# Leading pieces of the second unit's maxima: made ahead of the attention loop, or caught up inside its first twelve steps

## The chip, the cores and the metric

The kernel runs on one core of a Trainium2 chip. Five engines work beside each other and meet only at semaphores: PE (TensorE, matmuls, with PEld for the loading of the stationary operand), DVE (VectorE), ACT (ScalarE), POOL (GpSimd) and SP (SyncE, which here only issues DMAs). Each engine takes its instructions in order. The metric is the device time of one execution in microseconds. One execution was also recorded by the hardware profiler, and all times of single instructions come from that one.

## What is computed

Two independent heads, put side by side in the output. Head A is a long convolution (its kernel K is made from complex exponentials, the convolution is done by transforms). Head B is softmax attention without a mask, and it is in B that the change lies:

```python
def _B_ref(x, wqkv, wo):          # x [1, 2048, 448]
    H = 16; Dh = D // H           # 16 heads of 28
    qkv = (x @ wqkv).reshape(B, S, 3, H, Dh).transpose(2, 0, 3, 1, 4)
    q, k, v = qkv[0], qkv[1], qkv[2]
    scores = jnp.einsum("bhqd,bhkd->bhqk", q, k) * Dh ** -0.5
    p = _softmax(scores, axis=-1)
    o = jnp.einsum("bhqk,bhkd->bhqd", p, v)
    return o.transpose(0, 2, 1, 3).reshape(B, S, D) @ wo
```

All inputs and outputs are float32.

## The kernel before, in words

**Stages.** A first stage (lines 226 to 590) makes q, k and v and the seeds of head A's kernel, and ends with the row maxima of the first attention unit. Then one loop of NS = 256 steps (line 1045) does all of the attention, with the rest of head A spread over it as side jobs, and a tail finishes head A.

**Units and steps.** The 16 heads are four groups of four (G, HG). The 2048 query rows are four chunks of 512 (NQ). A unit u is one group and one chunk, 16 in all (NU); each has 16 steps (NK), one for every 128 keys. In a step, `s_mm` (line 753) makes the scores of 128 keys against 512 queries for each of the four heads (tile pss, a ring of three PSUM banks) and ACT turns each into p by an exponential; `pv_step` (line 760) multiplies the p of the step before with v into po.

**Maxima.** The exponential needs each row's maximum. It isn't subtracted afterwards: it is put as two extra rows into the query operand qhat, by `max_end` and `max_put` (lines 212 and 220: a PE transpose, two DVE operations that write mh, and two DMAs qhat<-mh), and the scores then come out with it taken off. So a unit's maxima must be finished before its first score. For that, `max_mm` (line 187) computes the scores of 128 query rows of one head against all 2048 keys once more, in four pieces kc = 0 to 3, each a matmul of 128x512 into one bank pm:

- kc 0: matmul with kdif (the difference of two halves of the keys), then ACT writes its relu into rl;
- kc 1: matmul with one of these halves, then DVE adds rl and takes the row maximum in one operation;
- kc 2 and 3: matmul with a quarter of the keys, then a DVE maximum (TENSOR_REDUCE).

The relu with the sum gives the elementwise maximum of both halves, so that three DVE passes do for four quarters. A unit needs 16 row blocks (i) of four pieces, 64 pieces. Step s of the loop makes the four pieces of block `sm = s + NK + LEAD` (blocks counted through all units), which is a unit and LEAD = 3 blocks ahead of the step itself. The first unit's maxima are made before the loop, and so are the three blocks of the second unit by which the loop is ahead (lines 906 to 908): 12 pieces. When a unit's last block is done, `max_join` and `max_end` follow.

**The order in a step** is written out by hand (line 34):

```python
ORDER = ('m0', 's0', 'm1', 's1', 'v', 'f', 'pv', 'f', 'v', 'k', 'm2', 's2', 'm3', 's3', 'v')
```

m is a piece of the maxima, s the scores of one head, pv the product with v. v is one DVE operation of head A (`vec`, from `g_powers`, tiles g and zg: nine per block, the first of them three short instructions). f is a side job of PE (`slot`, line 996): parts of head A's transforms (`u_part`, tiles ua, w to ub), the kernel's blocks (`k_mm`, tiles e, g to ko, and w, ko to yk), or what a finished unit still wants. k starts a block of head A's kernel (`k_begin`, `k_seed`) and hands POOL its next e operations. Within the loop all five engines keep exactly this program order (line 903).

**Banks.** PSUM's eight banks are ps_s with three for pss, ps_o with one for po, ps_g with one for zg, and three for pm. `w_tile` (line 125) hands the three out in turn, pm0, pm1, pm2, to the pieces of the maxima and to all side jobs alike. A matmul into a bank waits until what was there three takings before has been read out.

**Just before the loop** the order is: the first unit's maxima and their `max_end`, with the two puts on ACT's DMA queue; `load_sd(0)`, also on ACT's queue (sdb), and `load_sd(1)` and (2) on SP's; the twelve pieces; `k_seeds(0)` twice, which copies sdb on ACT into e and g for POOL and DVE; then step 0.

Of the kernel before, what the change touches and what calls it, by code (L numbers as in the profile page):

```python
# [26 lines left out]
NK = L // 128  # L27
# [4 lines left out]
NS = NU * NK  # L32
LEAD = 3
# [57 lines left out]
def body(ctx, tc, a, out):  # L91
# [5 lines left out]
    def pool(stack, name, bufs=1, space=None, side=None):  # L97
        kw = {} if space is None else {"space": space}
        if side:
            kw["side"] = side  # L100
        return stack.enter_context(tc.tile_pool(name=name, bufs=bufs, reuse_waits="tile", **kw))
# [23 lines left out]
    def w_tile():  # L125

        n_ring[0] += 1
        return ps_w[0].tile([128, CQ], F32, name=f"pm{n_ring[0] % ps_w[1]}")
# [16 lines left out]
    def load_k(g, j, p):  # L145
        if j == 0:
            t = k0_t if g == 0 else p.tile([128, HG, L], F32R, name="khat")
            kt_g[g] = [t[:, i] for i in range(HG)]
        for r in range(4):
            nc.sync.dma_start(kt_g[g][j][r::4, :].bitcast(F32), k_d[g][r % 2, 32 * j:32 * j + 32, :])  # L150
# [3 lines left out]
    def load_v(g, c):  # L154
        v_g[g, c] = t = v_p.tile([128, NK // NQ, HG, 32], F32, name="v", bufs=5)
        nc.sync.dma_start(t.rearrange("p t h e -> p t (h e)"), v_d[c][:, g])

    def load_kd(g, j, rows=range(4)):
        if 0 in rows:
            kd_g[g, j] = kd_p.tile([128, CQ], F32R, name=f"kdif{j}")  # L160
        t = kd_g[g, j]
        for r in rows:
            nc.sync.dma_start(t[r::4].bitcast(F32), kd_d[g][r % 2, 32 * j:32 * j + 32, :])

    def load_q(u, rows=range(4)):
        g, c = divmod(u, NQ)
        if 0 in rows:
            q_u[u] = q_p.tile([128, HG, CQ], F32R, name="qhat", bufs=3)
        t = q_u[u]
        for r in rows:  # L170
            nc.sync.dma_start(t[r::4].bitcast(F32), q_d[g][c][r // 2].rearrange("(j p) q -> p j q", j=HG))
# [15 lines left out]
    def max_mm(u, i, kc, ps=w_tile):  # L187

        if i == 0 and kc == 0:
            m_u[u] = q_p.tile([128, HG, 4, 3], F32, name="mx", bufs=2)  # L190
        j, t = divmod(i, 4)
        pm = ps()
        q, kt = q_u[u][:, j, t * 128:(t + 1) * 128], kt_g[u // NQ][j]
        mx = m_u[u][:, j, t, max(kc - 1, 0):max(kc - 1, 0) + 1]
        if kc == 0:
            nc.tensor.matmul(pm, q, kd_g[u // NQ, j], start=True, stop=True)
            rl_u[u, i] = kd_p.tile([128, CQ], F32, name="rl", bufs=2)
            nc.scalar.activation(rl_u[u, i], pm, AF.Relu)
        elif kc == 1:
            kb = kt.rearrange("p (c s n) -> p c s n", c=NQ, s=2)[:, :2, 1, :]  # L200
            nc.tensor.matmul(pm.rearrange("p (c n) -> p c n", c=2), q, kb, start=True, stop=True)
            rl = rl_u.pop((u, i))
            nc.vector.tensor_tensor_reduce(rl, pm, rl, 1.0, -3.0e38, ALU.add, ALU.max, mx)
        else:
            nc.tensor.matmul(pm, q, kt[:, kc * CQ:(kc + 1) * CQ], start=True, stop=True)
            nc.vector.tensor_reduce(mx, pm, axis=AX.X, op=ALU.max)
# [448 lines left out]
    def load_sd(b, queue=nc.sync):  # L655
        sds[b] = g_p.tile([128, SDF], F32, name="sdb", bufs=4)
        queue.dma_start(sds[b], sd_d[b // BO][b % BO])

    def k_seeds(b):

        if b not in es:
            es[b] = e = g_p.tile([128, 2, 16, N2], F32, name="e", bufs=2)
            nc.scalar.activation(e[:, :, :, :8], sds[b][:, :F_G].rearrange("p (c h e) -> p c h e", c=2, e=8), AF.Copy)
        else:
            g = g_p.tile([128, 2, 16, N1], F32, name="g", bufs=2)
            nc.scalar.activation(g[:, :, :, :4], sds[b][:, F_G:F_Z].rearrange("p (c h e) -> p c h e", c=2, e=4), AF.Copy)
            egs[b] = es.pop(b), g
# [85 lines left out]
    def s_mm(u, kt, j):  # L753
        pss = ps_s.tile([128, CQ], F32, name="pss")
        nc.tensor.matmul(pss, kt_g[u // NQ][j][:, kt * 128:(kt + 1) * 128], q_u[u][:, j, :], start=True, stop=True)
        p = kq_p.tile([128, CQ], F32, name="p", bufs=PB)
        nc.scalar.activation(p, pss, AF.Exp, scale=SCALE)
        return p
# [10 lines left out]
    def load_og(u):  # L769
        og_u[u] = og = kq_p.tile([128, G - 1, CQ], F32, name="og")  # L770
        nc.sync.dma_start(og, on_d[u % NQ][:G - 1].rearrange("g p q -> p g q"))
# [131 lines left out]
    nc.kept = KEPT["a"]  # L903
    for b in range(3):
        load_sd(b, nc.sync if b else nc.scalar)
    for i in range(LEAD):
        for kc in range(4):
            max_mm(1, i, kc)
    k_seeds(0)
    k_seeds(0)  # L910

# [84 lines left out]
    def slot(s_):  # L996
        n_slot[0] += 1
        if urgent and urgent[0][0] <= n_slot[0]:
            urgent.popleft()[2]()
        elif s_ >= NS and f_slot(s_, "s"):  # L1000
            pass
        elif p_due and p_due[0][0] <= s_:
            p_due.popleft()[1]()
        elif m_due and m_due[0][0] <= s_:
            m_due.popleft()[1]()
        elif u_due and u_due[0][0] <= s_:
            u_part(*u_due.popleft()[1:])
        else:
            f_slot(s_, "s") or f_slot(s_, "f")

    def k_seed(s_):
        b = k_due[0] if k_due else NB
        if b < NB and b not in egs and done["mm"] >= b - 2 and K0 + b * KP <= s_ + (1 if b in es else 2):
            k_seeds(b)
# [18 lines left out]
    def k_next():  # L1033

        if last[0] is not None and not powers["e"] and not powers["g"]:
            if last[0] + 3 < NB:
                load_sd(last[0] + 3)
            last[0] = None

    def vec():  # L1040
        if powers["g"]:
            powers["g"].popleft()()

    prev = None
    for s in range(NS):
        u, kt = divmod(s, NK)
        sm = s + NK + LEAD
        if s == 12 * NK:
            k0_st.close()
            f_p["s", 0] = f_p["s", 1] = pool(f0_st, "f0_p", side="right")  # L1050
            f_ready["s", 0], f_ready["s", 1] = s, NS
        if s >= 12 * NK and f_ready["s", 1] == NS and not (k_due or m_due or powers["g"] or powers["e"]):
            g_st.close()
            ps_st.close()
            ps_w[:] = pool(ps_st, "ps_f", 4, PSUM), 1
            f_ready["s", 1] = s + F1
        if kt == 12 and u // NQ == G - 1:
            load_og(u)
        late[0] = s + NK + LEAD > NS
        if u % NQ == NQ - 1 and u < NU - 1 and kt % 4 == 2:  # L1060
            load_v(u // NQ + 1, kt // 4)
        if sm < NS and sm // NK % NQ == NQ - 1 and sm % NK % 4 == 0 and sm % NK and sm // (NQ * NK) + 1 < G:
            load_kd(sm // (NQ * NK) + 1, sm % NK // 4 - 1)
        if sm < NS and sm % (NQ * NK) == 0 and sm:
            load_kd(sm // (NQ * NK), HG - 1)
        if kt % 4 == 1 and u % NQ == 1 and u // NQ + 1 < G:
            load_k(u // NQ + 1, kt // 4, k_pools[(u // NQ + 1) % 2])
        if kt == 2:
            if u + 2 < NU:
                load_q(u + 2)  # L1070
        ps = []
        for op in ORDER:
            if op[0] == "s":
                ps.append(s_mm(u, kt, int(op[1])))
            elif op[0] == "f":
                slot(s)
            elif op[0] == "v":
                vec()
            elif op == "k":
                k_next()  # L1080
                k_begin(s)
                k_seed(s)
                for _ in range(3):
                    if powers["e"]:
                        powers["e"].popleft()()
            elif op == "pv":
                if prev:
                    pv_step(*prev)
                    if prev[1] == NK - 1:
                        fin(prev[0], s)  # L1090
            elif sm < NS:
                max_mm(sm // NK, sm % NK, int(op[1]))
        for _ in range(FX if late[0] else 0):
            slot(s)
        if sm < NS and sm % NK == NK - 1:
            def end(un=sm // NK):
                max_end(un, w_tile())
                max_put(un)
            max_join(sm // NK)
            soon_slot(UG[0], end)  # L1100
        k_next()
        prev = (u, kt, ps)
    pv_step(*prev)
    fin(prev[0], NS)
    s = NS
# [63 lines left out]
```

## Time and profile before

| | us |
|---|---|
| median of three runs | 1278.88 |
| lowest and highest of them | 1276.07 and 1279.31 |
| the profiled execution | 1278.37 |
| its span, first to last instruction | 1276.6 |
| first score matmul of step 0 (from the span's start) | 228.65 |
| first score matmul of step 12 | 273.00 |

How to read the lines: times count from the span's start. PE, DVE, ACT, POOL and SP are the engines, a q behind a name is its instruction queue (waits, DMA issues). Almost all instructions carry L75, the line of a helper through which they are issued, so groups are told apart by their tiles: out<-in. In a row of the timeline stand start, duration, engine, operation, tiles, shape, how many, and in brackets the idle time before and what ended it. In a row of the windows stand the stretch, its length, then busy time and count of PE, PEld, DVE, ACT and POOL, the granted clock of TensorE, the share of the DMA engines and GB/s. In a row of the chain stand start, length and what held it.

### The profile page before, as it was taken

How to read it: one execution, taken by the hardware profiler on the slowest of the kernel's cores; microseconds unless marked ns; L12 is line 12 of the kernel's file. 1: busy time of each engine (PE TensorE's matmuls, PEld its weight loads, DVE VectorE, ACT ScalarE, POOL GpSimd, SP SyncE). 2: the span in 40 equal slices, each digit the busy share in tenths (PEclk: the TensorE clock that was granted, in tenths of full speed). 3: DMA queues.
4: the chain of work that ended last, by engine and by line, in shares of the span. 5: the costliest groups of instructions: out<-in, count | busy, mean ns of one | idle time of the engine just before them, and what ended most of it. 6: DMA issues, size and time to landing. Idle time of an engine off the chain costs nothing.

```text
span 1276.6 us, 33328 instructions
## 1 busy us (share of the span) xinstructions
PE 1223.9 (96%) x12641; PEld 699.3 (55%) x12641; DVE 923.0 (72%) x2106; ACT 967.5 (76%) x2162; POOL 846.2 (66%) x728
## 2 busy tenths in 40 slices
PE   7789887999999999999999999999999999999997
PEld 5667664555555555555555555555555545544433
DVE  6788866877777877877788888888897645645111
ACT  6878765788888888888878888888887666656452
POOL 2666750897788888878599999989995222324321
PEclk9889999899999999999999999999999999999999
DMA  7768699446564645375633133422324533657666
GB/s 216 244 223 288 233 304 346 113 93 186 160 149 113 168 119 168 113 235 167 176 94 104 49 88 97 154 81 71 88 54 156 179 131 135 204 170 228 198 170 167
DMA packets 200089, 205.36 MB, mean 161 GB/s; under 512 B 95992, under 2 KB 158520, under 8 KB 197880
## 3 DMA queue, kind: packets, MB, share of 16 engines
q1 hardware_dynamic: 199400, 202.63, 52.6%
q8 instruction: 100, 1.64, 0.5%
q10 hardware_dynamic: 528, 0.59, 0.2%
q14 instruction: 61, 0.50, 0.1%
HBM read 120.73 MB, written 82.18 MB: 159 GB/s over the span
## 4 chain that ended last, share of the span: by engine, by line
PE 75%; DVE 8%; POOL 6%; ACT 4%; issue 3%; DMA 3%; SPq 0%; ACTq 0%; POOLq 0%; DVEq 0%
PE pm L75 43%; PE pss L75 16%; PE po L75 16%; POOL e L75 2%; DVE tri L75 1%; ACT rl L75 1%; POOL qhat L75 1%; DVE mx L75 1%; DVE sg L75 1%; POOL eu L75 1%; ACT tri L75 1%; DVE px L75 1%; DVE qhat L75 1%; DVE hl L75 1%; DMA sd<-qhat 1%
## 5 line engine op out<-in xcount | busy, mean ns | idle before, releaser
L75 ACT ACTIVATE p<-pss 128x512 f32<-128x512 f32 x1024 | 561.0, 610 | 112.5 <-PE pss L75 107.2
L75 PE MATMUL pss<-qhat,khat 128*128 128x512 f32 x1024 | 403.2, 400 | 1.5 <-ACT p L75 1.4
L75 DVE TENSOR_REDUCE mx<-pm 128x1 f32<-128x512 f32 x480 | 308.6, 684 | 109.1 <-PE pm L75 107.2
L75 PE MATMUL pm<-khat,qhat 128*128 128x512 f32 x749 | 325.9, 438 | 6.4 <-ACT rl L75 4.2
L75 POOL TENSOR_TENSOR e<-e,sdb 128x256 f32<-128x256 f32 x168 | 201.8, 1201 | 110.6 <-ACT e L75 101.2
L75 PE MATMUL po<-p,v 128*32 128x512 f32 x2048 | 269.1, 594 | 0.0
L75 POOL TENSOR_TENSOR e<-e,eu 128x256 f32<-128x256 f32 x168 | 248.2, 1477 | 13.2
L75 PEld LDWEIGHTS pm<-khat,qhat 128*128 128x128 f32 x749 | 141.0, 189 | 201.9 <-ACT p L75 47.8
L75 DVE CUSTOM_DVE_ANT_0 rl<-pm,rl 128x512 f32<-128x512 f32 x259 | 178.3, 689 | 72.1 <-ACT rl L75 69.1
L75 PEld LDWEIGHTS pss<-qhat,khat 128*128 128x128 f32 x1024 | 190.6, 189 | 46.7 <-issue 10.8
L75 POOL TENSOR_TENSOR eu<-e,sdb 128x256 f32<-128x256 f32 x168 | 201.9, 1202 | 0.0
L75 POOL TENSOR_TENSOR p<-pr,pr 64x448 f32<-64x448 f32 x64 | 73.2, 1144 | 158.2 <-PE pm L75 132.8
L75 ACT ACTIVATE rl<-pm 128x512 f32<-128x512 f32 x259 | 156.6, 606 | 14.0 <-PE pm L75 8.4
L75 DVE TENSOR_TENSOR g<-g,zg 128x128 f32<-128x128 f32 x392 | 162.2, 414 | 3.4
L75 PE MATMUL pm<-kdif,qhat 128*128 128x512 f32 x249 | 100.5, 403 | 4.3 <-DVE xn L75 2.4
L75 PE MATMUL pm<-xh,khat 112*128 112x512 f32 x256 | 87.3, 425 | 4.9 <-DVE hl L75 1.8
L75 DVE TENSOR_TENSOR zg<-g,zg 128x128 f32<-128x128 f32 x224 | 88.0, 393 | 5.1
L75 PEld LDWEIGHTS pm<-e,g 128*32 128x32 f32 x3584 | 57.2, 109 | 43.4 <-issue 17.1
L75 DVE TENSOR_TENSOR pr<-pm,ub 128x448 f32<-128x448 f32 x64 | 37.0, 620 | 56.4 <-PE pm L75 42.0
L75 PE MATMUL pm<-e,g 128*32 128x64 f32 x3584 | 73.0, 222 | 1.8 <-POOL e L75 1.8
L75 ACT ACTIVATE y<-pm 128x448 f32<-128x448 f32 x48 | 26.5, 553 | 58.2 <-PE pm L75 36.2
L75 ACT ACTIVATE ub<-pm 128x224 f32<-128x224 f32 (+1 forms) x96 | 38.8, 449 | 39.7 <-PE pm L75 37.3
(134 smaller groups left out, 1461.8 us busy)
## 6 DMA issues: line engine op xcount, KB each, us to landing
sdb<-sd SPq DMA_DIRECT2D x55, 336.0 KB
qhat<-q SPq DMA_DIRECT2D x64, 256.0 KB
khat<-k SPq DMA_DIRECT2D x64, 256.0 KB
sd<-sg SPq DMA_DIRECT2D x8, 1456.0 KB
k<-hl SPq DMA_DIRECT2D x16, 512.0 KB
mw<-in_mw SPq DMA_DIRECT2D x16, 512.0 KB
sd<-qhat SPq DMA_DIRECT2D x8, 896.0 KB
yu_d<-ub SPq DMA_DIRECT2D x64, 112.0 KB
```

Source lines behind the costliest of these rows:

```text
L75: i = f(*args, **kw)
```

## The change

The twelve pieces ahead of the loop go. A counter `n_max` starts at the second unit's first piece (64), and `next_max` makes the next piece in order, whatever step it falls in. Each of the four m places of a step calls it once; at the end of the step it is called once more, as long as the counter is under `lead`. In steps 0 to 11 this is true, so these make five pieces, the fifth directly before the next step's m0 with no score matmul between; since five is not a multiple of four, the kind kc at each place moves on by one from step to step. After twelve steps the counter has reached the place that it has before the change, and from step 12 on a step makes its four pieces of block sm as before. The last pieces of a unit are made in the same step as before in all units.

```diff
@@ -903,9 +903,6 @@
     for b in range(3):
         load_sd(b, nc.sync if b else nc.scalar)
-    for i in range(LEAD):
-        for kc in range(4):
-            max_mm(1, i, kc)
     k_seeds(0)
     k_seeds(0)
...
@@ -1041,10 +1038,19 @@
+    n_max = [4 * NK]
+
+    def next_max(end=None):
+        n = n_max[0]
+        if n < 4 * NS and (end is None or n < end):
+            n_max[0] += 1
+            max_mm(*divmod(n // 4, NK), n % 4)
+
     prev = None
     for s in range(NS):
         u, kt = divmod(s, NK)
         sm = s + NK + LEAD
+        lead = 4 * sm + 4 if s >= 4 * LEAD else 4 * (s + NK + 1) + s + 1
...
@@ -1088,8 +1094,9 @@
-            elif sm < NS:
-                max_mm(sm // NK, sm % NK, int(op[1]))
+            else:
+                next_max()
+        next_max(lead)
         for _ in range(FX if late[0] else 0):
             slot(s)
```

## The prediction

> **What bounds the kernel now.** I read three views in this order: the page for the whole, the chain of waits around the start of the main loop, and the windows laid over its first twelve steps.
>
> ```profile
> PE 1223.9 (96%) x12641; PEld 699.3 (55%) x12641; DVE 923.0 (72%) x2106; ACT 967.5 (76%) x2162; POOL 846.2 (66%) x728
> ...
> PE 75%; DVE 8%; POOL 6%; ACT 4%; issue 3%; DMA 3%; SPq 0%; ACTq 0%; POOLq 0%; DVEq 0%
> ...
> 220.09 1.29 ACTq L75
> ...
> 222.07 0.61 ACT rl L75
> ...
> 222.72 6.13 PE pm L75 x10
> 228.85 0.43 PE pss L75
> ...
> 248.54 0.23 PE pss L75
> 248.77 0.23 PE pm L75
> ```
>
> TensorE holds three quarters of the chain that ends last. Before the loop that is another matter: at 222.72 the chain enters a block of pm matmuls (pieces made ahead) that lasts 6.13 us, and only then comes the first score matmul, pss. Inside the loop the chain goes from pm to pss in 0.23 us hops: there the matmul stream itself is the clock of the kernel.
>
> ```profile
> 228.65:231.22 2.57, 2.57 (x9) 2.05 (x8) 1.92 (x5) 2.08 (x5) 2.41 (x4) 0.70 0.51 108
> ...
> 234.31:237.62 3.31, 3.31 (x17) 1.50 (x16) 3.27 (x8) 2.80 (x7) 3.23 (x3) 1.00 0.36 139
> ...
> 249.31:253.54 4.23, 4.23 (x42) 2.28 (x40) 3.33 (x8) 3.83 (x9) 4.07 (x5) 1.00 0.61 132
> 253.54:256.59 3.05, 3.05 (x18) 1.58 (x16) 2.73 (x7) 2.47 (x7) 2.97 (x3) 1.00 0.75 149
> ...
> 268.75:273.00 4.25, 4.25 (x58) 2.29 (x56) 1.99 (x5) 3.36 (x9) 4.09 (x4) 1.00 0.50 116
> sum 44.35, PE 44.35 PEld 24.06 DVE 35.10 ACT 36.83 POOL 41.00; mean PE 3.70 PEld 2.01 DVE 2.92 ACT 3.07 POOL 3.42
> ```
>
> Each row is one step, cut at the first score matmul (time, then busy PE, PEld, DVE, ACT, POOL, then the granted clock); the rows cut out lie between, and the sum is over steps 0 to 11. PE is busy without a gap, so a bare step takes 3.05 us and one with side jobs 4.23. DVE has 35.10 of 44.35 us, 79%; in step 2 it has 3.27 of 3.31, and that step took 0.26 us more than the bare one with the same matmuls: the one place where DVE shows through.
>
> **The change, part by part.**
>
> *The twelve pieces leave the front.* Four matmuls each for three 128-row blocks, three ACT relus and nine DVE evacuations go. What they cost there is not 12 matmuls of time. The first score matmul also needs the first unit's negated maxima, which two DMAs on ACT's queue put into qhat.
>
> ```profile
> SPq L75 <- DMA qhat<-mh: 9.7, 1, 9.7
> ...
> 218.98 0.47 PE L75 MATMUL pm<-kdif,qhat 128*128 128x512 f32 x1
> ...
> 224.40 0.81 SPq L75 DMA_DIRECT2D sdb<-sd  x2
> ...
> 224.60:225.30 0.70, 0.70 (x3) 0.56 (x2) 0.30 (x2) 0.28 (x1) 0.00 (x0) 0.50 0.00 0
> ...
> 227.08 0.41 ACT L75 ACTIVATE e<-sdb 128x256 f32<-128x256 f32 x1
> ...
> 228.22 0.34 PEld L75 LDWEIGHTS pss<-qhat,khat 128*128 128x128 f32 x1
> ```
>
> The first piece, at 218.98, waits for no put and stays where it is. SP sits 9.7 us behind a qhat put and issues at 224.40, so one put has landed by then; from 224.60 to 225.30 the DMA engines move nothing (share 0.00), so the second put, and sdb for the first k block, have landed by 224.60. I let step 0's first score start at 224.6. Before, it starts at 228.65 (the cut of the windows). That is 4.0 us gained. Bounds: 4.2 (the put of 224.40) and 0.4, since the weight load at 228.22 waits for nothing the view shows and so proves no later landing.
>
> On ACT, k_seeds (e, g) now stands ahead of the first relu. With sdb there at 224.6, e takes 0.41 (its row) and g less; the relu of piece 0 then ends near 226, and the fourth piece, which wants that bank back, is five matmuls after 224.6 at half clock, near 226.7. No wait is charged. If e started only at 227.08 as before, that piece would wait some 1.5 us; it is in the range.
>
> *The clock.* The stretch before the loop runs at half clock:
>
> ```profile
> 216.55:219.96 3.41, 1.64 (x6) 0.57 (x4) 2.21 (x9) 0.63 (x2) 0.00 (x0) 1.00 1.04 401
> 219.96:223.37 3.41, 0.65 (x1) 0.29 (x1) 0.67 (x3) 0.60 (x1) 0.00 (x0) 0.50 1.06 345
> 223.37:226.79 3.42, 3.42 (x7) 1.72 (x6) 3.02 (x8) 0.80 (x2) 0.00 (x0) 0.50 0.60 184
> 226.79:230.20 3.41, 3.41 (x8) 2.31 (x8) 2.36 (x6) 1.99 (x5) 2.47 (x4) 0.50 0.80 224
> 230.20:233.60 3.40, 3.40 (x18) 1.86 (x18) 3.30 (x10) 3.25 (x7) 3.24 (x4) 1.00 0.74 239
> ```
>
> The granted clock (third column from the end) is 0.50 from 219.96 to 230.20. Before, the loop is in it for 1.55 us (228.65 to 230.20). If it returns at the same moment, the new loop is in it from 224.6, 5.6 us. Half of the 4.05 us more is lost: +2.0. The lead stage hardly paid for the half clock, since it waited on evacuations; loop steps pay it in full. Bounds: back one stretch earlier (226.79), 1.7 us less; one later, 1.7 more. PE starts in the middle of the 223.37 stretch, and seven matmuls there were not enough before, so I take 230.20.
>
> The Trainium skill (TensorE: Matmul & The Clock Gate, Part 1) says the full clock comes back after about 3.4 us of sustained matmuls, whenever these begin, and its closing list of aims wants no PE gap over about 3 us between bursts. This speaks against the change, whose PE waits from 219.45 (the end of the first piece) to 224.6; the trace had lost the clock by 219.96 anyway. By that rule alone the clock would be back at 228.0, the term would be about +0.9 in place of +2.0, and the sum 1.1 us lower; the rows do not agree that any 3.4 us do, because PE works from 222.72 and the clock returns 7.5 us later.
>
> *Twelve matmuls enter the loop.* Here PE has no gap, so each is paid in full:
>
> ```profile
> 248.04 0.50 PE L75 MATMUL pm<-khat,qhat 128*128 128x512 f32 x1
> ...
> 248.58 1.29 DVE L75 TENSOR_REDUCE mx<-pm 128x1 f32<-128x512 f32 x2 [0.71 <-PE pm L75]
> 248.61 0.40 PE L75 MATMUL pm<-khat,qhat 128*128 128x512 f32 x1
> ...
> 249.07 0.40 PE L75 MATMUL pm<-kdif,qhat 128*128 128x512 f32 x1
> ...
> 249.54 0.40 PE L75 MATMUL pm<-khat,qhat 128*128 128x512 f32 x1
> ...
> 249.78 0.41 DVE L75 TENSOR_TENSOR g<-g,zg 128x256 f32<-128x256 f32 x1
> ...
> 250.10 0.64 PE L75 MATMUL pm<-w,ko 128*32 128x128 f32 x16
> ...
> 257.33 0.28 DVE L75 TENSOR_TENSOR g<-g,zg 128x128 f32<-128x128 f32 x1
> ...
> 258.18 0.68 DVE L75 CUSTOM_DVE_ANT_0 rl<-pm,rl 128x512 f32<-128x512 f32 x1
> ```
>
> From 248.61 to 249.54 four hops (a pss stands between each two pieces) take 0.93 us: 0.233 each. Twelve cost +2.8. Bounds: 0, if PE had room the view hides, and 2.8.
>
> *Their evacuations meet the ring of three banks.* Pieces and side jobs share pm0 to pm2. Before, a step ends m2, m3 and the next step does m0, m1 and its first side job (f), which takes the bank that m3 had. After, the extra piece x stands between: m2, m3, x, m0, m1, f, and f takes x's bank. I lay x into the step of the rows above, at 249.07 where now m0 is. DVE runs the reduces of m2 and m3 from 248.58 to 249.87 (1.29), then a g operation if the step has one at its third place (about 0.33 of engine time, 0.41 with its tail), then x, 0.64: done at 249.87 + 0.33 + 0.64 = 250.84. f, at 250.10 before, would be at 250.33 with one matmul more; it waits 0.5. With the three short g operations of a block's beginning (257.33 to 258.18, 0.85) it waits 1.0. With none, or with x a relu on ACT, it is 0 to 0.2, and I take 0.
>
> Which case holds goes by the new order on DVE and PE. x is a DVE evacuation in all steps but 0, 4 and 8. First side jobs stand in steps 3, 4, 5, 6, 8, 9, 10, 11 and 12. One g operation ahead of x: into steps 3, 6 and 10, 0.5 each; a chain of a relu and its maximum in its place: into 11, 0.4; three: into 8 and 12, 1.0 each; into 4, 5 and 9, nothing. Sum +3.9. Behind the waiting f stand the four pv matmuls and the next scores on PE, and so ACT's exponentials: the whole step moves. Bounds: 0, if the evacuations keep up as they do before, and 8 steps of 1.0, 8. I take the list, since it is laid out on rows of these steps. DVE's total is not the limit: nine more evacuations of about 0.66 make 41.0 of some 47 us.
>
> *What stays.* From step 12 on, both orders are the same on every engine, and POOL's and SP's orders are the same throughout; the last step of unit 1's maxima stays in step 12. So what is won or lost by then stays to the end. POOL gets its first e some 2 us earlier, worth nothing, since PE waits for none of its results in these steps.
>
> **The sum.** -4.0 + 2.0 + 2.8 + 3.9 = +4.7 us. The profiled execution took 1278.37 us (span 1276.6 and 1.8 around it), 0.5 under the median 1278.88 of the three runs. Forecast: 1278.37 + 4.7 = 1283.1.
>
> **The rivals.**
>
> *The ring holds (not slower).* DVE has 9 us free in the twelve steps, and the side job could land late enough. Then the sum is -4.0 + 2.0 + 2.8 = +0.8: 1279.2. For it: no step but step 2 shows DVE in PE's way now. Against: x's bank is taken again after two matmul pairs, and the rows give DVE too little time for it.
>
> *The pieces are free (faster).* If PE's row, which counts modelled ends, hides room, the matmuls cost nothing and only start and clock are left: -2.0, 1276.4; with the clock back at 226.79, -3.7, 1274.7. The point from which it decides is the 0.233 us hop: if a step with five pieces lasts as long as one with four. Against: bare steps of 3.05 us leave no idle PE, and every other hop of the chain is a matmul.
>
> *The start does not move (slower).* The puts land later without the pieces in front, or ACT's e holds the first relu and exponentials to 227.08. The gain falls to 0.4 to 1.5 us, and the half clock costs less (about 0.5): -1.0 + 0.5 + 2.8 + 3.9 = +6.2, 1284.6; with the ring at its bound of 8, 1288.7. For it: e also waits on transfers of the stage before. Against: idle DMA engines from 224.60 on.
>
> **How the numbers follow.** About 0.3%, 3.8 us, is what a measurement can tell from no change, so slower begins at 1282.7. The forecast has 0.60, its own range 1281 to 1286, a sixth of it under 1282.7; the ring holds 0.20; the pieces are free 0.10, taken as faster; the start does not move 0.10. Slower: 0.50 + 0.10 = 0.60; the same: 0.10 + 0.20 = 0.30; faster 0.10. The range goes from 1278.5, just under the case without waits, to 1287.5, short of the worst bound.
>
> **What would show it.** The first pss at about 224.6, and the clock at 0.50 until about 230.2 (a stretch either way moves the time by 1.7). Steps 3 to 12 longer by 0.23 where no side job leads, and by 0.7 to 1.2 where it does, with PE or PEld idle behind DVE mx ahead of e,g and ua,w matmuls. The first score of step 12, at 273.0 before, at about 277.7. It is wrong if steps 3 to 11 grow by 0.23 alone, if the first pss is past 226, or if the shift at step 12 isn't the shift at the end.

## The result, and the profile after

| | us |
|---|---|
| after, median of five runs | 1283.71 (1283.18 to 1284.80) |
| before on the same chip, median of five runs | 1278.99 (1276.07 to 1279.44) |
| ratio, 95% interval | 1.0042 [1.0031, 1.0052] |
| the profiled execution after, and its span | 1283.71 and 1281.9 |

The change makes the kernel 4.7 us slower. The profiled pair differs by 5.34 (1283.71 - 1278.37). The page after, its busy times and the engines' shares of the chain:

```profile
PE 1221.6 (95%) x12641; PEld 694.2 (54%) x12641; DVE 921.4 (72%) x2106; ACT 967.6 (75%) x2162; POOL 846.9 (66%) x728
...
PE 74%; DVE 9%; POOL 5%; ACT 5%; DMA 3%; issue 3%; ACTq 0%; SPq 0%; POOLq 0%; DVEq 0%
```

The same instructions, and hardly a busy time has moved (PE 1223.9 before, 1221.6 after). What is new is time in which PE waits: DVE and ACT have each one per cent more of the chain. The timeline around the loop's start shows the first of these waits:

```profile
217.92 0.28 DVE L75 TENSOR_SCALAR mh<-pt 16x128 fp32r<-16x128 f32 x1 [0.45 <-PE pt L75]
...
218.28 2.01 ACTq L75 DMA_DIRECT2D qhat<-mh  x2
...
223.68 0.86 SPq L75 DMA_DIRECT2D sdb<-sd  x2
...
225.28 0.77 PE L75 MATMUL pss<-qhat,khat 128*128 128x512 f32 x1 [5.38 <-DMA qhat<-mh]
...
226.24 0.42 ACT L75 ACTIVATE e<-sdb 128x256 f32<-128x256 f32 x1 [9.72 <-DMA sdb<-sd]
...
226.76 0.58 ACT L75 ACTIVATE rl<-pm 128x512 f32<-128x512 f32 x1
...
227.24 1.07 ACT L75 ACTIVATE p<-pss 128x512 f32<-128x512 f32 x2
```

The first score waits for a put (qhat<-mh) until 225.28, 1.6 us after SP's own wait for the other put ended at 223.68. ACT then waits for sdb until 226.24, and the first relu and the first exponentials stand behind its two copies.

The mh operation at 217.92 is the mark from which I compare executions. It stood at 219.02 before: the first stage, whose code is the same, ended 1.1 us sooner in this execution. In the nine profiled executions with an unchanged first stage (the two kernels, and seven of the experiments below) it lies between 217.36 and 219.15, so that is chance. Behind this mark the first score comes at 7.36 in place of 9.63 us: 2.27 gained.

The windows after, cut at the first score matmul of each step as in the prediction (time, busy PE, PEld, DVE, ACT, POOL, the granted clock, DMA share, GB/s); steps 0, 2, 6, 7, 8, 11 and the sum:

```profile
225.28:229.23 3.95, 3.95 (x10) 2.74 (x10) 1.86 (x5) 2.99 (x8) 2.34 (x4) 0.52 0.92 250
...
233.10:236.40 3.30, 3.30 (x19) 1.69 (x17) 3.13 (x7) 2.67 (x7) 3.22 (x3) 1.00 0.85 274
...
249.96:255.03 5.07, 5.07 (x42) 2.31 (x41) 3.28 (x7) 4.10 (x10) 4.83 (x7) 1.00 0.63 143
255.03:258.82 3.79, 3.79 (x18) 1.61 (x17) 3.72 (x10) 3.16 (x8) 3.71 (x3) 1.00 0.48 117
258.82:264.44 5.62, 4.82 (x59) 2.40 (x57) 4.04 (x11) 3.35 (x8) 3.47 (x2) 1.00 0.01 2
...
273.27:278.17 4.90, 4.90 (x58) 2.40 (x57) 2.62 (x7) 3.67 (x10) 4.74 (x4) 1.00 0.33 89
sum 52.89, PE 51.56 PEld 25.45 DVE 39.60 ACT 39.85 POOL 43.61; mean PE 4.30 PEld 2.12 DVE 3.30 ACT 3.32 POOL 3.63
```

Twelve steps take 52.89 us in place of 44.35, 8.54 more, where twelve matmuls at 0.233 make 2.8. The busy PE of these rows counts modelled ends, and so hides most of the waits: in step 6 no gap shows, though the step lasts 0.84 longer for one matmul more. Step by step, in us (the steps' lengths, and the shift of the next step's start against before, both counted from the mark):

| step | before | after | more than a matmul | shift behind it |
|---|---|---|---|---|
| 0 and 1 | 5.66 | 7.83 | 1.70 | -0.10 |
| 2 | 3.32 | 3.29 | -0.26 | -0.13 |
| 3 | 3.95 | 4.81 | 0.63 | +0.74 |
| 4 | 3.49 | 4.01 | 0.29 | +1.26 |
| 5 | 4.25 | 4.73 | 0.25 | +1.75 |
| 6 | 4.23 | 5.07 | 0.61 | +2.59 |
| 7 | 3.05 | 3.79 | 0.51 | +3.34 |
| 8 | 4.43 | 5.61 | 0.95 | +4.52 |
| 9 | 4.25 | 4.74 | 0.26 | +5.01 |
| 10 | 3.48 | 4.09 | 0.38 | +5.62 |
| 11 | 4.25 | 4.91 | 0.43 | +6.27 |
| 12 (no fifth piece) | 4.24 | 5.17 | 0.93 | +7.21 |

So the start is used up by step 2, and steps 3 to 12 lose 7.34: nine matmuls, 2.10, and 5.24 of waits. The shift then stays: +7.21 behind step 15, +6.96 at step 240, +6.44 at the end. With the 1.1 of the first stage taken off, that is the 5.34 between the two executions.

The timeline of step 8 shows what the largest of them is:

```profile
258.95 0.28 DVE L75 TENSOR_TENSOR g<-g,zg 128x128 f32<-128x128 f32 x1
...
259.09 0.19 PEld L75 LDWEIGHTS pm<-khat,qhat 128*128 128x128 f32 x1 [0.30 <-DVE mx L75]
...
259.26 0.29 DVE L75 TENSOR_TENSOR zg<-g,zg 128x128 f32<-128x128 f32 x1
...
259.43 0.40 PE L75 MATMUL pss<-qhat,khat 128*128 128x512 f32 x1
...
259.59 0.29 DVE L75 TENSOR_TENSOR g<-g,zg 128x128 f32<-128x128 f32 x1
259.80 0.68 DVE L75 TENSOR_REDUCE mx<-pm 128x1 f32<-128x512 f32 x1
...
260.63 0.65 PE L75 MATMUL pm<-e,g 128*32 128x64 f32 x32 [0.81 <-DVE mx L75]
```

The fifth piece's maximum stands on DVE behind three short g operations and ends at 260.48; the first side job (e,g) wants its bank and leaves PE idle for 0.81 us. This is the wait that the prediction drew. The row of 259.09 is another one, which it did not draw: m1 of the same step waits 0.30 us with its weight load.

### The profile page after: what moved, and what is told of

Its sections match the earlier page's. It is cut to its first block, busy times and chain, and to the rows that moved or that the text cites. A ratio compares the mean times of both kernels' runs of the same rounds, so it can differ in the third digit from the quotient of the medians.

```text
span 1281.9 us, 33331 instructions
## 1 busy us (share of the span) xinstructions
PE 1221.6 (95%) x12641; PEld 694.2 (54%) x12641; DVE 921.4 (72%) x2106; ACT 967.6 (75%) x2162; POOL 846.9 (66%) x728
## 4 chain that ended last, share of the span: by engine, by line
PE 74%; DVE 9%; POOL 5%; ACT 5%; DMA 3%; issue 3%; ACTq 0%; SPq 0%; POOLq 0%; DVEq 0%
PE pm L75 42%; PE pss L75 16%; PE po L75 16%; DVE mx L75 1%; POOL e L75 1%; DVE tri L75 1%; POOL qhat L75 1%; ACT rl L75 1%; ACT tri L75 1%; DVE sg L75 1%; DVE rl L75 1%; POOL p L75 1%; DVE hl L75 1%; ACT p L75 1%; DVE px L75 1%
```

## The experiments

All ratios stand against the kernel before on the same chip. "Steps 3 to 12" is their growth against before in the profiled execution.

### The start alone

The kernel before without the twelve pieces ahead; they aren't caught up either, so that the maxima of the first three blocks of the second unit are left out (zeros in their place):

```diff
-    for i in range(LEAD):
-        for kc in range(4):
-            max_mm(1, i, kc)
+    m_u[1] = q_p.tile([128, HG, 4, 3], F32, name="mx", bufs=2)
+    nc.gpsimd.memset(m_u[1][:, 0, :LEAD, :], 0.0)
```

> The twelve pieces are not made ahead and not caught up either (the maxima of unit 1's first three row blocks are left at zero), so that only the earlier start is left. Ring theory (the loss is made inside the twelve steps, where the fifth piece's bank is wanted back too early; the start itself gains): first score about 7.4 us after the first mh operation as in the changed kernel (9.6 before), half clock in the loop 2.3 us longer, together -2.3 + 1.1 = -1.2 us: 1277.8. Restart theory (the loss is the cold, empty start): slower than before, +3 or more: 1282.

Measured: 1276.69 against 1278.22, 0.9982 [0.9972, 0.9991]. The first score comes 7.50 behind the mark, 2.13 sooner; steps 0 to 3 then give back 1.25 (14.18 in place of 12.93), and the shift stays near -0.87 through step 12. All that the front had to give is 1.5 us by the medians, where the prediction's first two terms (-4.0 and +2.0) made 2.0.

The kernel before with the two puts on SP's queue in place of ACT's:

```diff
-        max_put(0, nc.scalar)
+        max_put(0)
```

> The kernel before, with the first unit's two puts issued from SP's queue and not from ACT's. In the profile before, the first relu of the twelve pieces waits on ACT until 222.07 behind the issue of two puts and sdb. Start theory (the pieces ahead end late because ACT issues DMAs first): first relu at about 0.5 to 1.5 us behind the first mh in place of 3.05, the twelve pieces end 1.5 to 2.5 us sooner, and the first score is at 7.4 to 8.1 us in place of 9.6; the half clock then covers that much more of the loop: -0.8 to -1.2 us, 1277.2 to 1277.6. If the puts land later from SP's queue, 0 or worse.

Measured: 1276.27 against 1277.78, 0.9990 [0.9981, 0.9999]. The first score stands 8.78 behind the mark, 0.85 sooner with all twelve pieces still in front of it (expected were 7.4 to 8.1). Its first relu:

```profile
220.90 0.60 ACT L75 ACTIVATE rl<-pm 128x512 f32<-128x512 f32 x1 [3.62 <-PE pm L75]
```

That is 2.21 behind the mark. Before, the first relu stood on ACT behind ACT's own issuing of three DMAs until 222.07, 3.05 behind the mark (rows ACTq and rl of the chain in the prediction). It starts 0.84 sooner here, and the pieces and the first score move by as much. In neither kernel does the first score wait for a put: the pieces held it, and the queue on which the puts are issued held the pieces.

A middle way, LEAD = 2: eight pieces ahead and none caught up, with the last piece of each unit one step later.

> The kernel before with LEAD = 2: eight pieces ahead of the loop, four pieces in every step, and each unit's maxima and puts one step later. If a piece ahead costs what it takes to evacuate it (2.3 us for four, as between two relus of the twelve), the first score is 2.3 us sooner, the longer half clock takes 1.1 back, and the four pieces come back at the end of the maxima as +0.9: -0.3 us, 1278.7. If the puts of the later units then land too late, up to 2 us in each of 14 units: over 1285.

Measured: 1279.75 against 1277.78, 1.0009 [1.0001, 1.0018]. A miss: the first score came 1.58 sooner (8.05) and the shift stayed near -0.7 through step 12, but step 15, in which the second unit's maxima are now finished, took 5.34 in place of 4.24. The shift was then +0.1, still -0.2 at step 240, and +2.2 at the end of the profiled execution: most of the loss comes in the last sixteen steps, and what makes it there was not followed up.

### The matmul, the bank and the reader

The kernel before (twelve pieces ahead) with one more matmul at the end of steps 0 to 11, into a bank of the ring, which nobody reads:

```diff
+        if s < 4 * LEAD:
+            pm = w_tile()
+            nc.tensor.matmul(pm, q_u[1][:, 0, :128], kt_g[0][0][:, 2 * CQ:3 * CQ], start=True, stop=True)
```

> The kernel before, with one more 128x512 matmul at the end of each of steps 0 to 11, at the fifth piece's place and into the ring of three, whose result nobody reads. Ring theory: the matmuls alone cost 12 x 0.233 = +2.8 us, with no waits since the bank is free at once: 1281.8. Free-pieces theory: PE has room, 0: 1279.0. Restart theory: the start is as before, so 0 to +2.8, it does not say.

Measured: 1286.58 (1283.84 to 1288.24), 1.0057 [1.0044, 1.0071], where 1281.8 was expected: a miss. In its profile steps 3 to 12 grow by 4.22, where the matmuls make 2.1. A matmul without a reader costs 0.47 (4.22 for nine of them), twice its time. Its step 6 shows where, in the timeline:

```profile
250.53 0.50 PE L75 MATMUL pm<-kdif,qhat 128*128 128x512 f32 x1
250.87 0.40 PE L75 MATMUL pss<-qhat,khat 128*128 128x512 f32 x1
...
251.13 0.19 PEld L75 LDWEIGHTS pm<-khat,qhat 128*128 128x128 f32 x1 [0.30 <-DVE mx L75]
251.13 0.50 PE L75 MATMUL pm<-khat,qhat 128*128 128x512 f32 x1
...
251.47 0.40 PE L75 MATMUL pss<-qhat,khat 128*128 128x512 f32 x1
```

m1 starts in the same moment as its weight load (251.13), m0 and m1 take 0.50 in place of 0.40, and the score behind each comes after 0.34 us, not 0.23. The banks go round by threes: before, m0 takes the bank of the last side job, which is long free, and m1 that of m2. With one taker more, m0 takes m2's and m1 takes m3's, which are younger, and which DVE gives back just as they are wanted. That is soon enough for the matmul, but too late for its weight load to be fetched ahead.

The rival to this is that a matmul costs more than 0.233 wherever it is put. So the same matmul into a bank that m3 takes anyway, directly ahead of m3's own:

```diff
+            if kc == 3 and twice[0]:
+                nc.tensor.matmul(pm, q, kt[:, 2 * CQ:3 * CQ], start=True, stop=True)
             nc.tensor.matmul(pm, q, kt[:, kc * CQ:(kc + 1) * CQ], start=True, stop=True)
...
+        twice[0] = s < 4 * LEAD
```

> The kernel before, with one more matmul in each of steps 0 to 11 that goes into m3's own bank just ahead of m3 and is overwritten by it, so that no bank of the ring is taken. Turn theory (a fifth taker of three banks makes the next m0 and m1 take banks that were let go too late for their weight loads to be fetched ahead, 0.25 us a step without any evacuation, as the run of the unread matmuls lets one think): steps 3 to 11 are longer by 0.23 each and no more, +2.8 by step 12. Price theory (a lone matmul between others costs 0.49 us wherever it goes): +0.49 a step, +5.8.

Its timeline at the same place:

```profile
250.22 0.39 PE L75 MATMUL pss<-qhat,khat 128*128 128x512 f32 x1
250.22 0.19 PEld L75 LDWEIGHTS pm<-khat,qhat 128*128 128x128 f32 x1
250.45 0.40 PE L75 MATMUL pm<-khat,qhat 128*128 128x512 f32 x1
```

The weight load starts 0.23 us ahead of its matmul again, without a wait, and steps 3 to 12 grow by 1.80, nine times 0.20. The same matmul costs 0.20 in a bank that is already taken and 0.47 where it takes a turn of the ring. The medians stand less clearly (1281.81 against 1277.78, 1.0037 [1.0023, 1.0051]): the runs fall into two groups, 1279.96 to 1282.82 and 1284.49 to 1285.90, the profiled one (1280.21) in the lower; on that see the last section.

The waits of PEld for DVE's maxima, over steps 1 to 11, in the waits view of before, after, this kernel and the one with the extra bank (us in total, times, longest):

```profile
PEld pm L75 <- DVE mx L75: 3.3, 8, 0.8
```

```profile
PEld pm L75 <- DVE mx L75: 10.5, 24, 0.8
```

```profile
PEld pm L75 <- DVE mx L75: 1.6, 4, 0.8
```

```profile
PEld pm L75 <- DVE mx L75: 6.6, 22, 0.4
```

Twenty-two loads wait where nobody even reads the extra bank, four where there is no extra bank. The twenty-two are the loads of m0 and m1 in each of the eleven steps, 0.30 us each.

The unread matmul again, now with a reader, a DVE maximum into a scratch tile:

```diff
+            nc.vector.tensor_reduce(kq_p.tile([128, 1], F32, name="scr", bufs=2), pm, axis=AX.X, op=ALU.max)
```

> As the run with the unread matmuls, but each is evacuated by a DVE maximum, all twelve of them (the changed kernel has nine on DVE and three on ACT), and the twelve pieces ahead stay. Ring theory: +2.8 for the matmuls and 5 to 7 us of PE waits for DVE in steps 1 to 12 on top: +8 to +10, 1287 to 1289, with first score and clock as before. Restart theory: no more than the matmuls, +2.8: 1281.8.

Measured: 1288.13, 1.0075 [1.0063, 1.0088]. Steps 3 to 12 grow by 7.80, 3.6 more than without the reader; 5.7 us of waits of PEld, in seven places, are now for this scratch. A reader behind x makes the first side job wait, as predicted, and that comes on top of the turn.

Then the changed kernel with its fifth piece at another place, directly ahead of m2, where two more pieces stand between it and the next side job:

```diff
         for op in ORDER:
+            if op == 'm2' and s < 4 * LEAD:
+                next_max()
...
-        next_max(lead)
```

> The changed kernel, with the fifth piece made right before m2 in place of the end of the step, so that the next first side job takes m3's bank again and DVE gets the piece when it is idle. Ring theory: the waits of the side jobs go (about 4 of 5.5 us), the rest stays: 1279 to 1280.5. If the loss is the evacuation work as such, or the start, the place does not matter: 1283.7 as the changed kernel.

Measured: 1282.46, 1.0029 [1.0018, 1.0040]. Steps 3 to 12 grow by 4.84 in place of 7.34; step 8, in its windows:

```profile
260.21:264.99 4.78, 4.78 (x59) 2.33 (x57) 4.05 (x11) 3.11 (x8) 3.06 (x2) 1.00 0.01 3
```

It was 5.62 with the fifth piece at the end. The gain by step is 0.25, 0.31, 0.83, 0.32 and 0.79 in steps 3, 6, 8, 10 and 12, and nothing in 4, 5, 7, 9 and 11: the steps that the prediction named, but for 11, and 2.5 us together. What is left beside the matmuls, 4.84 - 2.1 = 2.7, is put down to the turn of the ring. The median gained only 1.3 thousandths, and 1282.46 misses the expected 1279 to 1280.5. In the profiled execution steps 0 and 1 took 9.22, 1.4 longer than after: 0.47 of that goes with e, which starts 1.43 behind the first score in place of 0.96 (why e counts is told further down, with the clock), and the other 0.93 comes with a half clock that lasted one stretch longer, to 232.80.

### The first two steps

The prediction charged them with the half clock. To take it away, matmuls that nobody reads go into the changed kernel: 6 ahead of `max_end` and 20 behind the puts, in banks of the ring.

```diff
+        for _ in range(6):
+            nc.tensor.matmul(w_tile(), kt_g[0][0][:, :128], kt_g[0][0][:, :CQ], start=True, stop=True)
         max_join(0, 2)
...
+    for _ in range(20):
+        nc.tensor.matmul(w_tile(), kt_g[0][0][:, :128], kt_g[0][0][:, :CQ], start=True, stop=True)
     k_seeds(0)
```

> The changed kernel, with 6 unread matmuls ahead of the first unit's max_end and 20 behind its puts, so that PE stays busy until the puts have landed. Clock theory (the half clock in the first steps costs half of the time that it lasts in the loop, 3.8 us in the changed kernel): the clock never drops or is back before the first score, which stays at about 7.4 us behind the first mh, steps 0 and 1 are 1.9 us shorter together, the rest as in the changed kernel: 1281.8. If ACT's and DVE's work sets the first steps, no gain: 1283.7. If the clock drops all the same, the 20 matmuls delay the first score by up to 1 us: 1284.5.

Measured: 1283.29 against 1277.78, 1.0040 [1.0028, 1.0052]. Inconclusive: the matmuls ran at full clock and were done at 221.44, PE idled 2.6 us and the clock fell after all, from 224.67 to 228.08, in the loop's first microseconds. With 32 in place of 20 it stays:

> The changed kernel with 6 unread matmuls ahead of the first unit's max_end and 32 behind its puts (20 ended 2.8 us before the first score, and the clock dropped in that gap). Clock theory: PE is busy until the puts have landed, the clock stays at full, the first score stays at 7.4 to 7.9 us behind the first mh, and steps 0 and 1 together last 5.9 to 6.3 us in place of 7.8: 1.9 us less than the changed kernel, 1281.5 to 1282. If ACT and DVE set these two steps, no gain: 1283.3 to 1283.7.

Measured: 1285.20 against 1278.35, 1.0055 [1.0042, 1.0068]. The granted clock is full from the first stage into the loop, and steps 0 and 1 take 8.37 us together, 0.54 more than after had at half clock. The timeline of its step 0:

```profile
227.09 0.39 PE L75 MATMUL pss<-qhat,khat 128*128 128x512 f32 x1
...
227.64 0.42 ACT L75 ACTIVATE e<-sdb 128x256 f32<-128x256 f32 x1 [10.77 <-DMA sdb<-sd]
227.97 0.29 ACT L75 ACTIVATE g<-sdb 128x128 f32<-128x128 f32 x1
228.16 0.58 ACT L75 ACTIVATE rl<-pm 128x512 f32<-128x512 f32 x1
228.64 1.07 ACT L75 ACTIVATE p<-pss 128x512 f32<-128x512 f32 x2
228.80 0.49 PE L75 MATMUL pm<-khat,qhat 128*128 128x512 f32 x1 [1.32 <-ACT rl L75]
```

PE stands idle for 1.32 us behind a relu that is 0.58 long: the relu stands behind e and g, and e waits for sdb. That the half clock alone paces these steps has fallen. The new theory is that ACT does, by sdb. If so, with the two copies moved into step 0, to just ahead of `k_begin` (their first reader), the first relu no longer stands behind sdb:

```diff
-    k_seeds(0)
-    k_seeds(0)
...
             elif op == "k":
+                if s == 0:
+                    k_seeds(0)
+                    k_seeds(0)
                 k_next()
```

> The changed kernel with the 6 + 32 unread matmuls of the run before (full clock throughout), and with ACT's two copies of the first sdb (e and g) moved from ahead of the loop to the place in step 0 where the kernel's first block begins, behind four scores and two exponentials. ACT theory (in steps 0 and 1 PE waits for the first relu, which stands behind e, which waits for sdb): the relu of the first piece no longer stands behind sdb, so steps 0 and 1 together last 6.6 to 7.2 us in place of 8.37 with the same unread matmuls, the shift from step 2 on is smaller by 1.2 to 1.8, and the ratio to the kernel before falls by about 0.001. Rival: what is slow in steps 0 and 1 is the fifth piece and its bank; then they stay at about 8.3 us and the shift stays. A third way: e and g now stop ACT in the middle of step 0 behind sdb, and the loss is only moved into steps 0 and 1 by one place; then the sum of both is the same within 0.3 but step 1 is the longer one.

In its timeline the relu starts at once:

```profile
224.10 0.39 PE L75 MATMUL pss<-qhat,khat 128*128 128x512 f32 x1
224.30 0.60 ACT L75 ACTIVATE rl<-pm 128x512 f32<-128x512 f32 x1 [9.43 <-PE pm L75]
...
224.79 1.08 ACT L75 ACTIVATE p<-pss 128x512 f32<-128x512 f32 x2
...
225.75 0.43 ACT L75 ACTIVATE e<-sdb 128x256 f32<-128x256 f32 x1
...
230.82 0.50 PE L75 MATMUL pm<-khat,qhat 128*128 128x512 f32 x1 [0.80 <-DVE mx L75]
```

Steps 0 and 1 take 2.53 + 4.54 = 7.07, 1.30 less than with the copies in front, and the shift stays 1.3 smaller through the following steps. That is the ACT theory's forecast. The time was 1285.70 against 1279.50, 1.0051 [1.0037, 1.0064], and so says nothing about 1.3 us: the interval overlaps that of the run before. Step 1 now has a wait of 0.80 behind DVE's maxima.

The changed kernel with its fifth piece ahead of m2 and 6 and 32 unread matmuls, for what the ring costs without the half clock:

> As the run with 32, and the fifth piece right before m2 in place of the end of the step. If clock, side jobs' waits and turn of the ring are separate terms, their sums add: of the changed kernel's +7.2 us at step 13 against the first mh, 1.9 go with the clock and 2.5 with the side jobs' waits, +2.8 stay: 1278.8 to 1280. If the clock's 1.9 us only hides other waits, 1281 or more.

Measured: 1281.14 against 1278.35, 1.0034 [1.0022, 1.0047]. Steps 3 to 12 grow by 4.85 (4.84 without these matmuls), so the turn is neither the clock's nor chance. Steps 0 and 1 take 7.62 in place of 9.22. Of these 1.60 us, 0.67 go with e, which starts 0.76 behind the first score in place of 1.43; at most 0.93 is left for the 7.0 us of half clock in the loop by which the two executions differ. The expected sum did not come out: it gave the clock 1.9 us and asked for a shift of +2.8 at step 13 and 1278.8 to 1280. The shift there is +4.96, about the +7.2 of the changed kernel less the 2.5 of the side jobs alone, and the median lies in the range of the rival, in which the clock's 1.9 us only hide other waits.

### A version that is faster than both

The kernel before, the puts on SP's queue, and 18 unread matmuls that keep PE at full clock: 6 ahead of `max_end`, 6 behind the puts, and 6 among the twelve pieces, these in banks of pss, so that the pieces' ring keeps its turn.

```diff
+        for _ in range(6):
+            nc.tensor.matmul(w_tile(), kt_g[0][0][:, :128], kt_g[0][0][:, :CQ], start=True, stop=True)
         max_join(0, 2)
...
-        max_put(0, nc.scalar)
+        max_put(0)
...
+    for _ in range(6):
+        nc.tensor.matmul(w_tile(), kt_g[0][0][:, :128], kt_g[0][0][:, :CQ], start=True, stop=True)
     for i in range(LEAD):
         for kc in range(4):
             max_mm(1, i, kc)
+            if kc % 2:
+                nc.tensor.matmul(ps_s.tile([128, CQ], F32, name="pss"), kt_g[0][0][:, :128], kt_g[0][0][:, :CQ],
+                                 start=True, stop=True)
```

> A version that may beat both: the kernel before with the first unit's puts on SP's queue and unread matmuls to keep PE busy (6 ahead of max_end, 6 behind it, 6 among the twelve pieces, these in the score's banks). Clock theory: full clock when the first score starts, so the 1.1 us that the half clock costs the run with the puts on SP's queue alone go, and the twelve pieces, no longer at half clock, end up to 0.8 us sooner: 1275 to 1276 against about 1278. If the clock drops all the same or the unread matmuls hold the pieces up, 1276 to 1278.

Its windows from the first stage's end into the loop:

```profile
216.00:221.00 5.00, 4.93 (x18) 2.92 (x17) 2.29 (x9) 0.60 (x1) 0.00 (x0) 1.00 1.03 378
221.00:226.00 5.00, 4.78 (x17) 2.73 (x17) 4.67 (x11) 2.65 (x6) 1.89 (x3) 1.00 1.02 312
```

Full clock throughout, and the pieces stay ahead, where they fill the time in which the puts travel. Measured: 1275.38 (1274.54 to 1277.84) against 1278.35, 0.9979 [0.9971, 0.9988]. The puts alone gave 0.9990; the two intervals overlap, but in the traces the shift from step 3 on is -2.2 to -2.0 here and -0.7 to -0.5 there.

## Why the prediction was right, and where it wasn't

The forecast, +4.7 and 1283.1, met +4.7 and 1283.71. Its terms did not all meet theirs:

| term | forecast | found |
|---|---|---|
| start | -4.0 | -2.27 |
| steps 0 to 2 beside their matmuls ("clock") | +2.0 | +1.44, set by sdb |
| twelve matmuls | +2.8 | +2.8 at 0.233; 0.20 each in a bank already taken |
| waits in steps 3 to 12 | +3.9 | +5.24 |
| sum at step 13 | +4.7 | +7.2 |
| step 13 to the end | 0 | -0.8 |
| first stage, by chance | - | -1.1 |

*The start: right mechanism, too large by 1.7.* From SP's issue at 224.40 and idle DMA engines behind it the prediction took both puts as landed by 224.6. After, SP's issue stands at 223.68, 5.76 behind the mark, and the first score, held by a put, at 7.36: one put landed 1.6 us behind the other's signal. The idle DMA engines (share 0.00, 5.58 to 6.28 behind the mark) stand in that one execution only. The same stretch after:

```profile
223.50:224.20 0.70, 0.00 (x0) 0.00 (x0) 0.00 (x0) 0.00 (x0) 0.00 (x0) 0.50 1.06 325
```

In the twelve experiments the share there is 1.01 to 1.12, also where the code up to that point is that of before. And in the three of them that keep the front with its twelve pieces whole (the unread matmul, the same with its reader, the matmul in m3's bank) the first score comes 10.26 to 10.42 behind the mark, so that the 9.63 of before is an early one. The bounds ran from 0.4 to 4.2, and the value was taken close to the upper one. "The first pss past 226" was one of the marks of being wrong; in before's time (9.63 - 7.36 taken from 228.65) it came at 226.38.

*The clock: a term of nearly the right size, for another reason.* The half clock did last to 11.18 behind the mark, as in before, so the forecast of the clock itself held, and the loop had 3.8 us of it against 1.55. But that is not what the steps paid for. From e's start to the first score of step 2 it is 6.87 us after, with the clock at half for the first 2.9 of them, and 6.86 in the kernel with 32 unread matmuls, at full clock all the time; with 20 it is 6.87 too. So step 2 starts when it does because of when e starts, which is when sdb lands, and the half clock after added nothing that shows. Only where it lasted to 232.80, with the fifth piece ahead of m2, is it 7.80 (6.87 for the same kernel at full clock). The prediction saw e and g ahead of the first relu and charged nothing for them: it had sdb landed by 224.6 with e right behind, and e started at 226.24. Taking the copies out of the way gave 1.30 at full clock; what was not measured is the same at half clock. For the same reason the earlier first score was worth nothing by step 2 (a shift of -0.10): what followed it in steps 0 and 1 waited for sdb. That the term came out near +2.0 is luck.

The Trainium skill (TensorE: Matmul & The Clock Gate, Part 1) also says that the window over which the gate looks runs freely and does not start with the matmuls. The trace agrees: the clock changes only at the ends of stretches of 3.41 us (in before it is at half from 219.96 to 230.20, in after from 218.86 to 229.10, 10.24 each, three stretches). The prediction read the page's 3.4 us without this part; the return at 229.10 with PE starting at 225.28, 3.8 us, comes of a stretch that happened to begin 0.4 us later:

```profile
225.68:229.10 3.42, 3.42 (x9) 2.25 (x9) 1.73 (x4) 2.86 (x8) 2.21 (x4) 0.50 0.93 260
229.10:232.51 3.41, 3.35 (x17) 1.44 (x16) 3.31 (x10) 2.59 (x6) 3.25 (x4) 1.00 0.47 113
```

*The side job behind x: right mechanism, too large.* The list had 0.5 for steps 3, 6 and 10 (found 0.63, 0.61, 0.38), 0.4 for 11 (0.43), 1.0 for 8 and 12 (0.95, 0.93). That both sums are 3.9 is luck, since the numbers found hold the turn of the ring as well. By the kernel with x ahead of m2 the side jobs' wait itself is 2.5 in all: 0.25 to 0.32 in steps 3, 6 and 10, 0.83 and 0.79 in 8 and 12, and nothing in 11.

*The turn of the ring: missed.* The prediction asked only who takes x's own bank, and put nothing at 4, 5 and 9 ("0 to 0.2, and I take 0"). Found: 0.29, 0.25 and 0.26, and 0.51 in the bare step 7 (0.25 there with the unread matmul; the other half goes with the reader and was not taken apart). A fifth taker also makes m0 and m1 take younger banks, and a bank that comes free just in time for the matmul is too late for the weight load ahead of it. The unread matmul shows this without any reader, the matmul in m3's bank shows that it isn't the matmul. Over steps 3 to 12 it costs 2.1 without a reader; with readers, in the kernel with x ahead of m2, 2.7 stay. It is the term that the sum lacked.

*The rivals.* The pieces are not free (0.20 at least), the ring does not hold, and the start did move, though by half. What the third rival named, ACT's e in front of the first relu, is what was found in steps 0 and 1. That step 12's shift would be the end's held to 0.8. That the median met the forecast to 0.6 is owed to the terms' errors going against each other: 1.7 less gain and 1.3 more waits, against 0.6 less in steps 0 to 2, 0.8 in the later steps, and a first stage 1.1 shorter.

## What to carry to other kernels

An added taker of a ring of PSUM banks can cost the other takers behind it (here m0 and m1), not only the one that gets its bank: count three takings back for each, and want the bank free early enough for the weight load, which here starts 0.23 us before its matmul. Work that stands in front of a wait for a DMA is nearly free as long as the transfer is under way: before moving it, find the transfer that lands last, each one by itself and in more than one execution, and what the next engine has queued in front of its first useful instruction.

## What the hardware showed beside that

How dense the matmuls of a stretch of 3.41 us must be to bring the full clock back can't be read from their count. In before (windows in the prediction) 7 matmuls of 512 columns in the stretch of 223.37 did not, 8 in the next did; after, the 9 of the rows above did. With the fifth piece ahead of m2, 6 did not:

```profile
225.98:229.39 3.41, 2.87 (x6) 1.73 (x7) 1.02 (x3) 2.15 (x6) 1.58 (x3) 0.50 0.92 279
229.39:232.80 3.41, 3.41 (x11) 1.88 (x14) 3.30 (x9) 2.87 (x6) 3.25 (x4) 0.50 0.64 164
```

That execution had half clock for a whole stretch more. In the kernel with 6 and 20 unread matmuls 8 were enough. But so were 7 in the kernel with the scratch maximum, where the clock is full from 227.26 on:

```profile
223.85:227.26 3.41, 3.41 (x7) 1.62 (x7) 2.84 (x6) 1.08 (x2) 0.00 (x0) 0.50 1.05 363
```

The same holds for the 7 from 226.22 to 229.63 in the kernel with the matmul in m3's bank. The busy PE of the stretch doesn't decide either: it is 3.42 of 3.42 in before, where 7 did not bring the clock back. What does decide stays open.

The full clock can also be lost again near the end. The windows of the kernel with the unread fifth matmul:

```profile
1235.99:1239.40 3.41, 1.78 (x16) 0.94 (x20) 0.00 (x0) 2.06 (x4) 0.00 (x0) 1.00 1.10 280
1239.40:1242.80 3.40, 3.40 (x22) 1.10 (x14) 0.39 (x2) 0.10 (x1) 2.08 (x1) 0.51 1.09 346
1242.80:1246.20 3.40, 3.40 (x30) 1.36 (x29) 1.08 (x3) 2.16 (x5) 0.00 (x0) 0.98 0.93 201
```

Near the loop's end, one stretch with 1.78 us of busy PE is followed by one at half clock, and the shift of this execution goes from +6.1 at step 240 to +8.35 at the end. Part of that is the wait that empties the first stretch: PE stands 1.35 us behind a transfer (zi<-z, until 1238.94) that after holds it for 0.36. From the end of that wait to the next step's first score it is 4.54 us, in place of 2.93 after. Four of the profiled executions had such a stretch at half clock (this one, the one with the scratch maximum, and those with 6 and 32 unread matmuls but for the last); the profiles of before and after had none. These four grew by 2.2 to 3.3 us behind step 240, wait and clock together, which may be what parts the runs of 1280 and 1285 of one kernel. That was not shown, since only one execution of each was profiled, and LEAD = 2 lost 2.4 us there without such a stretch. In an execution of 1280 us it is as large as most of the terms here, which is why the steps were compared in the traces, and the medians only for the verdict.
